# One chain of small matrices for two batches instead of two, and the whole instruction order replaced

## The chip, the cores and the metric

The kernel runs on one core of one Trainium2 chip. Its time is the device time of an execution in microseconds (us); the number that counts is the median over the runs of a kernel. The engines are TensorE (PE, matmuls and transposes through it; PEld is its weight loads), VectorE (DVE), ScalarE (ACT), GpSimd (POOL) and SyncE (SP, which here only issues DMAs).

## The reference

Four batches, four heads, 1088 tokens, head size 32. The first block is attention with a sketched second-degree kernel; its output, as a matrix of 1088 x 128 for each batch, goes through a second block that mixes tokens with two 1088 x 1088 matrices.

```python
a = einsum('rd,bhsd->bhsr', S1, x); b = einsum('rd,bhsd->bhsr', S2, x)      # x is q, then k; r = 8
phi(x) = einsum('bhsi,bhsj->bhsij', a, b)                                   # 64 features
kv = einsum('bhsf,bhsd->bhfd', phi(k), v);  z = sum of phi(k) over s
x = (phi(q) @ kv) / (phi(q) . z + 1e-6)                                     # heads side by side: 128 columns
theta = x @ w_theta
y = w_tok_r @ (x * cos(theta)) + w_tok_i @ (x * sin(theta))
u = x + y
out = u + max(u @ w_ch, 0)
```

The denominator can come close to zero, so the kernel forms it in two words (a rounded part and a rest). That is what most of the small matrices are for.

## The kernel before

**The plan.** The kernel does not issue its work as it is written. Each step is recorded by `op` (L133) as an operation: an engine (P, V, A, G, S for PE, DVE, ACT, POOL, SP), an assumed duration, a function that emits its instructions, and the tiles that it writes and reads. The string `ORDER` (L29 to L67) lists the numbers of all operations in one sequence, found outside the kernel by a search. `lay` (L207) goes through it once with the assumed costs; from that it takes which buffer of a class each tile gets (22 "big" tiles, 5 "zs", 8 PSUM banks and so on) and a start time for each operation. `issue` (L273) then emits the operations in that sequence, so each engine's instructions stand in the order of the string. Between the operations `first` and `last`, where the plan sees PE idle, it emits "spins" (`spin`, L434): matmuls on an idle tile whose result nobody reads, one for each 0.2 us of planned gap.

**The work.** For each batch b:

- `load` (L659) brings k, q and v in. For batches 1 to 3 k is loaded a second time (`loadh`, L720).
- `key_sums` (L683): the sum of squares of k (ACT), a grid for rounding, k rounded to bf16 (`keys`, DVE), the rest k minus rounded (DVE). For batches 1 to 3, POOL adds the rounded words into the second copy of k by an accumulating DMA (`join`, L396; big<-hf). PE then forms for each head the product of the rounded words (`sums`, 9 steps) and of the rests with that second copy (`rest`, 9 steps; batch 0 has two products there instead). ACT copies them out (`halves`).
- `chain` (L838): from these 32 x 32 matrices a chain of small steps, each a short hop from engine to engine: DVE `split` in two words, PE product with the sketch, ACT copy, DVE `split_t`, PE product with a block matrix (`second`), DVE `norms`, PE product with ones, DVE `cut` (11 instructions), POOL `whole`. Its result (tiles mv and mf) is needed by `levels`. A chain may take several batches side by side: the tiles are then wider and some steps have other forms.
- `kfeatures` (L769): transposes of k (kT), its features (kf), their outer product on DVE and the sum with v on PE (kv), nine chunks in three groups. `chain_out` (L955) spreads kv.
- `query_scale`, `query_slices` (L997, L1021): q transposed on PE (qT), scaled by ACT, cut into f16 and a rest on DVE (q0).
- `levels` (L1050): nine PE steps give the features of q; DVE forms the denominator (`den`).
- `outputs_x` (L1129): outer products of the features (DVE, num, L384 g<-lv), transposed on PE (L1155), copied by ACT (L1159), multiplied with kv; then theta, its phase on DVE, sine and cosine on ACT (L1197 to L1203) and the product z = x * (cos, sin) on DVE.

Each of the 17 blocks of token weights (`row`) is loaded as 64-bit words and turned into fp32 by two ACT and two DVE instructions (L646 to L654). Batches 0 and 1 are mixed row by row (`mix`, PE). Batches 2 and 3 share a form with seven products (`winograd`, products 1 to 7; POOL adds weight blocks by DMA, L1328). Each output is finished with one more matmul and stored by SP, in four DMAs of 32 partitions (L1283) or, for the last 128 columns, in one (L1297).

**What the change touches.** `CHAINS` (L71) lists the batches that go through a chain together: batch 0 alone, batch 1 alone, 2 and 3 together. The loop near the end of the kernel goes through it: for the entry with batch 0 the features of k come after the chain, and `last` (the last operation before which spins are emitted) follows it. `read_small` (L452) loads the two sketch matrices; the plan gives that load a cost of 0.25. Right at the start, ACT runs one Sin on a tile `warm` (L444), before which its function table is loaded.

Of the kernel before, what the change touches and what calls it, by code (L numbers as in the profile page):

```python
# [26 lines left out]
TINY = 2.0**-60  # L27
UP = 256.0
ORDER = """  # L29
    0 1 35 12 5 13 10 11 107 14 53 15 16 18 54 108 57 55 101 19 58 20 47 48 59 17 3 4 60 61 62 63 64 65 66 38 67  # L30
    68 21 138 142 125 50 144 36 102 79 95 69 49 70 71 56 72 40 73 74 22 80 81 309 96 311 147 23 51 75 24 126 145
    7 250 257 261 28 127 82 39 97 128 129 251 98 25 8 99 103 310 143 312 104 105 139 76 77 78 140 31 263 192 193
    146 41 307 308 166 84 119 120 32 85 33 37 131 266 313 109 86 148 149 267 132 150 151 110 111 167 168 314 186
    100 344 268 269 152 153 87 88 205 209 345 106 112 154 244 9 347 113 133 187 42 188 134 26 264 89 2 245 34 90
    91 189 43 285 135 198 199 194 195 141 92 93 155 238 156 157 270 271 272 273 158 274 159 160 161 262 162 163
    6 211 164 165 286 287 121 239 29 122 27 114 190 315 123 346 171 348 200 201 94 364 424 116 428 425 426 429
    432 214 233 427 215 216 359 202 430 44 360 169 431 433 434 435 234 235 288 236 252 316 206 333 172 436 117
    366 327 124 437 438 196 45 253 173 207 210 439 328 217 118 174 175 440 317 339 83 441 442 365 325 170 176
    326 443 318 319 320 321 191 130 136 115 444 334 177 331 265 178 445 323 197 453 52 137 240 324 246 446 341
    241 332 30 213 247 179 203 204 180 335 336 454 460 449 322 46 340 450 447 218 219 242 220 221 222 258 275  # L40
    276 342 277 278 279 448 456 455 457 349 394 451 248 458 212 452 280 350 343 351 259 181 467 281 535 536 469
    531 470 537 532 463 459 533 282 283 534 527 528 529 538 461 530 539 223 224 225 226 227 228 254 464 476 183
    540 182 462 229 230 231 468 471 465 352 473 541 472 474 466 184 284 542 232 475 477 478 543 353 354 544 355
    243 545 546 547 548 484 249 255 256 549 356 384 483 492 493 485 185 386 361 479 480 556 481 260 486 494 385
    552 553 550 551 357 559 560 557 558 554 563 561 555 571 562 208 564 565 482 358 362 367 487 374 566 567 578
    570 572 489 289 573 574 575 576 363 488 368 329 579 369 495 290 568 580 569 581 370 371 496 497 375 291 577
    292 582 586 490 641 642 643 491 588 377 583 293 589 372 376 584 618 619 595 585 294 620 295 296 297 644 645
    379 646 380 381 621 590 622 596 623 373 419 330 396 395 592 591 298 498 668 669 670 303 382 421 383 671 672
    673 674 675 378 664 665 420 397 237 300 404 387 666 587 593 409 422 597 388 598 647 648 649 650 411 624 594
    423 406 305 410 405 389 667 398 412 676 599 600 601 602 299 301 391 407 413 408 390 603 604 499 392 393 399  # L50
    400 401 500 414 306 836 402 403 415 677 651 652 678 501 502 416 679 417 503 504 505 506 302 680 418 507 681
    508 515 682 683 840 509 337 684 685 688 690 338 686 687 730 726 727 731 732 728 521 729 865 722 723 724 653
    304 835 654 510 869 733 605 625 839 626 627 628 629 691 725 834 689 692 693 734 735 736 694 695 737 696 655
    630 631 738 739 740 741 742 743 632 698 746 748 697 699 744 747 700 656 701 511 512 705 657 707 703 749 658
    708 709 702 711 745 606 633 713 750 751 704 752 753 516 814 815 715 706 795 796 797 816 710 714 607 513 712
    817 798 755 804 837 754 756 716 717 777 779 780 863 719 799 781 818 819 718 522 868 768 770 800 759 761 720
    771 772 805 762 820 757 782 763 806 774 838 867 841 773 807 808 809 810 811 758 721 760 634 767 769 514 764
    801 893 608 864 765 635 766 831 776 775 778 783 784 832 861 802 851 852 821 853 854 833 891 862 523 524 855
    856 822 857 803 860 880 858 785 525 926 889 881 882 890 859 907 894 866 883 884 885 659 892 636 886 786 929
    930 870 823 827 787 788 789 790 609 895 928 791 792 793 610 908 887 896 794 871 872 873 909 910 932 911 912  # L60
    874 875 876 877 517 518 913 914 888 915 828 931 842 965 933 916 934 843 844 845 927 878 879 948 846 847 949
    950 920 939 848 849 850 812 935 937 813 637 897 638 639 936 526 611 612 613 951 940 924 952 953 954 898 899
    900 901 902 964 938 941 942 943 944 829 640 955 903 956 519 824 520 825 826 977 987 988 925 660 945 946 947
    661 830 662 663 960 904 905 966 989 614 906 615 967 968 969 616 961 617 921 917 918 919 970 971 972 973 957
    974 922 923 975 990 962 978 979 991 958 959 976 997 998 992 980 993 999 994 995 963 1000 996 981 982 983 984
    985 986 1006 1008 1007 1009 1001 1002 1010 1003 1004 1005
"""  # L67
WARM = 0
FILL = 5.0
SPINS = 8  # L70
CHAINS = ((0,), (1,), (2, 3))  # L71
QPOOL = (False,) * 4
KEEP = (2, 3)
KEEP_CLS = "big"
# [245 lines left out]
def kernel(  # L320
# [13 lines left out]
    S, DM = out.shape[1], out.shape[2]  # L334
# [122 lines left out]
    if wide:  # L457
        st = fixed((NS,), I64, "st")
        y = fixed((NS,), I32, "sy")
        z = fixed((NS,), I32, "sz")  # L460
        op("V", 0.1, lambda: V.memset(st().bitcast(F32), 0.0), [st], [])
        op("S", 0.25, read_small, [st], [], lk=3)

        def words():
            w = st().bitcast(I32).rearrange("p (n t) -> p n t", t=2)
            return w[:, :, 0], w[:, :, 1]

        op("A", 0.25, lambda: A.activation(sp()[:, 0], words()[1].bitcast(F32), AF.Prelu, scale=2.0**-112,
                                           alpha=-(2.0**32)), [(sp, 0)], [st])

        def unpack():
            wl = words()[0]
            x = sp()[:, 0].bitcast(I32)
            ts(x, x, 3, ALU.logical_shift_left)
            stt(x, wl, 29, x, ALU.logical_shift_right, ALU.bitwise_or)
            ts(y(), x, -(1 << 23), ALU.bitwise_and)
            ts(z(), wl, 0x1FFFFFFF, ALU.bitwise_and)

        op("V", 0.85, unpack, [(sp, 0), y, z], [st], lk=2)
        op("A", 0.25, lambda: A.activation(sp()[:, 1], z(), AF.Copy, scale=2.0**-52), [(sp, 1)], [z])  # L480
        vop(NS, lambda: tt(V, sp()[:, 1], sp()[:, 1], y().bitcast(F32), ALU.mult), [(sp, 1)], [y])
    else:
        op("V", 0.2, lambda: V.memset(sp(), 0.0), [sp], [])
        op("S", 0.25, read_small, [(sp, 0)], [], lk=3)

    def powers(mfn, m, n, name):

# [1013 lines left out]
```

## Time and profile before

| | us |
|---|---|
| runs | 221.52, 222.49, 222.84 |
| median | 222.49 |
| the profiled execution | 222.86 |
| its span, first to last instruction | 221.1 |
| PE busy | 212.8 |
| DVE busy | 167.0 |
| ACT busy | 114.9 |
| granted PE clock | 1.000 of full speed |

The span is the time between the first and the last instruction; some 1.8 us of the execution lie around it. Lines are given as in this kernel (L384 and the like); in the changed kernel all lines stand one lower. A line can be that of a helper: L404 is any matmul, L384 any DVE or POOL instruction with two tensors. Matmuls overlap and their ends are modelled, so a busy PE need not be PE at its peak.

### The profile page before, as it was taken

Reading aid. Unit: us, or ns where it says so; the run is one execution under the profiler, and the core shown is the slowest. Engines: PE = TensorE matmul, PEld = TensorE weight load, DVE = VectorE, ACT = ScalarE, POOL = GpSimd, SP = SyncE. Lnnn points to the kernel's source line nnn. Section 1 sums busy time; section 2 is a strip of 40 time slices with the busy share of each in tenths; the row PEclk is TensorE's granted clock in tenths of the full one; section 3 lists DMA queues with packets and bytes.
Section 4 is the critical chain, followed back from the end, with each engine's and each line's share of the span. In section 5 each row is a group of like instructions: output and inputs, shape, how many; then the busy total and the mean of one; then the engine's idle time right before and its main releaser. Section 6 shows DMA issues by size and latency. Waiting matters only on the chain.

```text
span 221.1 us, 5129 instructions
## 1 busy us (share of the span) xinstructions
PE 212.8 (96%) x2066; PEld 160.8 (73%) x2066; DVE 167.0 (76%) x360; ACT 114.9 (52%) x237; POOL 45.5 (21%) x81
## 2 busy tenths in 40 slices
PE   7999998999999999999999999999999999999993
PEld 3786987777776757686666685778888787788772
DVE  2899897999899999899999969953899005324951
ACT  3988657989699798949740042377930000000000
POOL 1168260101200000100040083000273165030000
PEclk9999999999999999999999999999999999999999
DMA  6999999985509008948862069411098489772673
GB/s 183 411 424 319 394 418 362 418 270 211 205 9 369 30 0 268 373 170 260 345 115 41 0 104 178 73 20 20 0 185 139 80 149 180 122 111 34 100 115 69
DMA packets 26987, 40.19 MB, mean 182 GB/s; under 512 B 18260, under 2 KB 19284, under 8 KB 24788
## 3 DMA queue, kind: packets, MB, share of 16 engines
q1 hardware_dynamic: 22212, 30.30, 40.0%
q0 software_dynamic: 4752, 9.57, 24.4%
q8 instruction: 16, 0.26, 0.4%
q14 instruction: 7, 0.06, 0.1%
HBM read 28.07 MB, written 2.23 MB: 137 GB/s over the span
## 4 chain that ended last, share of the span: by engine, by line
PE 80%; DVE 5%; ACT 5%; SPq 3%; DMA 3%; issue 2%
PE ps L404 73%; SPq L1283 3%; DMA big<-k_l 2%; PE ps L1188 2%; PE ps L1155 2%; PE ps L792 2%; ACT big L649 2%; PE ps L435 1%; DVE lv L384 1%; DVE g L384 1%; DMA out<-g 1%; PE ps L1035 1%; ACT big L699 1%; DVE big L391 1%; ACT big L1003 1%
## 5 line engine op out<-in xcount | busy, mean ns | idle before, releaser
L404 PE MATMUL ps<-big,zs 128*128 128x384 f32 (+4 forms) x366 | 102.8, 426 | 0.4 <-DVE big L384 0.4
L404 PEld LDWEIGHTS ps<-big,zs 128*128 128x128 f32 x366 | 65.6, 190 | 27.6 <-DVE big L384 1.6
L1267 ACT COPY g<-ps 128x384 f32<-128x384 f32 (+1 forms) x6 | 2.6, 464 | 44.6 <-DVE g L1279 32.0
L384 DVE CUSTOM_DVE_ANT_0 big<-big,big 128x2176 uint16<-128x2176 uint16 x17 | 21.5, 1285 | 0.3
L647 ACT ACTIVATE big<-zs 128x1088 f32<-128x1088 f32 x17 | 20.6, 1215 | 2.3 <-DMA zs<-w_tok 1.8
L649 ACT ACTIVATE big<-zs 128x1088 int32<-128x1088 uint32 (+1 forms) x18 | 20.8, 1167 | 1.1 <-DVE big L384 1.1
L404 PE MATMUL ps<-mf,big 128*128 128x96 f32 x72 | 14.6, 296 | 0.9 <-issue 0.9
L384 DVE TENSOR_TENSOR zs<-ps,g 128x768 f32<-128x768 f32 (+2 forms) x20 | 12.3, 629 | 3.6 <-ACT g L1201 2.2
L391 DVE SCALAR_TENSOR_TENSOR big<-ps,even,big 128x256 f32<-128x256 f32 (+1 forms) x10 | 4.8, 493 | 12.6 <-PE ps L404 12.6
L404 PE MATMUL ps<-big,big 128*32 128x32 f32 (+2 forms) x320 | 14.1, 220 | 0.2 <-issue 0.2
L1328 POOL DMA_DIRECT2D big<-zs x8 | 7.0, 1132 | 34.7 <-PE ps L404 29.4
L1328 POOL DMA_DIRECT2D big<-big x8 | 9.2, 1638 | 19.7 <-issue 19.7
L404 PEld LDWEIGHTS ps<-big,big 128*32 128x32 f32 (+1 forms) x320 | 10.3, 118 | 3.4 <-issue 1.5
L398 POOL DMA_DIRECT2D g<-big x6 | 7.8, 1433 | 23.4 <-ACT g L1267 23.4
L1295 ACT COPY g<-ps 128x128 f32<-128x128 f32 x2 | 0.5, 265 | 23.0 <-PE ps L1293 22.0
L388 DVE TENSOR_SCALAR big<-big 128x1088 int32<-128x1088 int32 x17 | 12.1, 719 | 0.0
L404 PEld LDWEIGHTS <-hf 128*32 128x32 bf16 (+1 forms) x252 | 10.8, 99 | 1.7 <-issue 0.5
L435 PE MATMUL ps<-idle 128*128 128x384 bf16 x39 | 10.6, 398 | 1.3 <-POOL idle L437 1.3
L404 PEld LDWEIGHTS ps<-mf,big 128*128 128x128 f32 x72 | 10.9, 191 | 1.1 <-issue 1.1
L384 DVE TENSOR_TENSOR g<-lv 128x768 f32<-128x768 f32 x12 | 11.1, 953 | 0.3
L404 PE MATMUL ps<-w,big 128*128 128x128 f32 x76 | 10.9, 280 | 0.4 <-ACT g L1295 0.4
L404 PEld LDWEIGHTS ps<-w,big 128*128 128x128 f32 x76 | 9.9, 192 | 1.5 <-ACT g L1295 0.6
(199 smaller groups left out, 399.6 us busy)
## 6 DMA issues: line engine op xcount, KB each, us to landing
zs<-w_tok SPq DMA_DIRECT2D x17, 1088.0 KB, 5.6
big<-k_l SPq DMA_DIRECT2D x7, 576.0 KB, 8.1
big<-q_l SPq DMA_DIRECT2D x4, 576.0 KB, 15.6
big<-v_l SPq DMA_DIRECT2D x4, 576.0 KB, 8.0
big<-big POOLq DMA_DIRECT2D x8, 272.0 KB, 6.1
big<-zs POOLq DMA_DIRECT2D x8, 272.0 KB, 3.9
zs<-big POOLq DMA_DIRECT2D x8, 272.0 KB, 5.7
big<-hf POOLq DMA_DIRECT2D x3, 576.0 KB, 9.9
```

The costliest lines, as they stand in the source:

```text
L384: eng.tensor_tensor(out=o, in0=a, in1=b, op=f)
L388: (eng or V).tensor_scalar(out=o, in0=a, scalar1=s1, scalar2=s2, op0=op0, **kw)
L391: (eng or V).scalar_tensor_tensor(out=o, in0=a, scalar=s, in1=b, op0=op0, op1=op1)
L398: op("G", 1.05, lambda: G.dma_start(dst(), src(), accum_op=ALU.add), w, r, chan=chan)
L404: T.matmul(o, lhs, rhs, start=start, stop=stop, skip_group_check=True)
L435: T.matmul(nowhere(), idle()[:, 0:P], idle(), start=True, stop=True, skip_group_check=True)
L647: op("A", 0.22 + n * 0.0009, lambda: A.activation(dfn(), words_of(raw(), n)[1].bitcast(F32), AF.Prelu, scale=2.0**-112, alpha=-(2.0**32)), ...
L649: op("A", 0.22 + n * 0.0009, lambda: A.activation(stp(), words_of(raw(), n)[0].bitcast(U32), AF.Copy, scale=2.0**-29), [stp], [raw])
L792: T.transpose(tr()[:, i * P:(i + 1) * P], kx()[:, g * GC + i].rearrange("p h d -> p (h d)"), ident())
L1155: T.transpose(tr()[:, i * P:(i + 1) * P], qp()[:, i * H + 2 * n:i * H + 2 * n + 2].rearrange("p h i j -> p (h i j)"), ident())
L1283: SY.dma_start(out[b, t0 - o:t0 + w, f * SQ:(f + 1) * SQ].rearrange("(c j) i -> j c i", j=SQ), ot()[f * SQ:(f + 1) * SQ, :o + w].rearrange ...
L1328: op("G", 1.05, lambda i=i: G.dma_start(dst[0](i), x[0](i), accum_op=ALU.add), [dst[1](i)], [x[1](i)], chan=ADD_FLY3)
```

## The change

```diff
 ORDER = """
-    0 1 35 12 5 13 10 11 107 14 53 15 16 18 54 108 57 55 101 19 58 20 47 48 59 17 3 4 60 61 62 63 64 65 66 38 67
...
+    0 1 35 53 12 13 14 2 10 38 126 57 15 16 58 17 18 54 59 132 127 138 7 84 151 60 61 62 63 88 64 19 20 65 85 21
...
-CHAINS = ((0,), (1,), (2, 3))
+CHAINS = ((0, 1), (2, 3))
...
-        op("S", 0.25, read_small, [st], [], lk=3)
+        op("S", 0.9, read_small, [st], [], lk=3)
...
-        op("S", 0.25, read_small, [(sp, 0)], [], lk=3)
+        op("S", 0.9, read_small, [(sp, 0)], [], lk=3)
```

Batches 0 and 1 go through one chain. Since operations are numbered as they are recorded, the numbers of the new string name other operations than those of the old one; the sequence is a new one throughout. The cost of the small load only enters the plan.

What the built programs hold, before and after: PE 39 and 42 spins, and four matmul calls fewer in the chain; DVE 362 and 345 instructions; ACT 229 and 225, among them one table load before and two after; POOL 86 and 84; SP the same 79. All other instructions are the same in number and form. The order of the loads on SP:

```
before: k0 small w2 k1 q0 k3 k2 k1again q1 v0 row1 q2 q3 k3again row5 row4 v1 v2 k2again row0 v3 row2 row11 ...
after:  k0 small k1 k1again q0 k3 k2 q3 w2 q1 q2 row1 v0 row0 row2 v1 row9 v2 k3again row5 k2again v3 row6 ...
```

The first operations on POOL (the number is the batch; "join" is the accumulating DMA):

```
before: idle grid0 blocks scaled square2 join1 sliced square2 grid1 blocks sliced chain0 join3 blocks join2 chain1 ...
after:  idle blocks grid0 join1 scaled square2 sliced grid1 sliced square2 blocks chain(0,1) blocks join2 join3 ...
```

PE up to batch 0's levels, without the repetitions:

```
before: kT0 sums0 kT1 rest0 qT0 kT3 kf1 kf0 rest0 kT2 qT0 kT1 sums3 kf0 chain0 sums1 kT2 kv0 kT3 kf1 kf2
        chain0 kT2 kf2 chain0 kT3 rest1 sums3 kf1 qT1 kf2 levels0 ...   (chain1 follows behind levels0)
after:  kT0 kT1 sums0 rest0 kT1 kf0 qT0 kf0 kf1 rest0 sums1 qT0 kf0 kT1 kT2 kf1 kT3 rest1 kf2 kT3 chain(0,1)
        kT2 qT3 chain(0,1) chain(0,1) kf2 kv0 kf1 kf2 kT3 levels0 ...
```

At the end PE had the 128-column parts of product 4 mixed with the others; in the new order the part for columns 288 to 416 comes alone, last. The Sin on `warm` is ACT's second instruction before, and stands behind 49 others after.

## The prediction

> **What bounds the kernel now.** I read the page first, then the chain of work that ended last, then the waits of TensorE (PE) and VectorE (DVE), then the timeline of the engines up to 92 us.
>
> ```profile
> span 221.1 us, 5129 instructions
> PE 212.8 (96%) x2066; PEld 160.8 (73%) x2066; DVE 167.0 (76%) x360; ACT 114.9 (52%) x237; POOL 45.5 (21%) x81
> ...
> PE   7999998999999999999999999999999999999993
> ...
> DVE  2899897999899999899999969953899005324951
> ```
>
> PE is busy almost throughout, so what can be won is time in which PE runs idle-tile spins (L435) or waits. The digits of DVE say where: 9 of 10 up to about 155 us.
>
> ```profile
> 46.29 0.38 DVE lv L384
> ...
> 46.69 1.83 DVE g L384 x2
> ...
> 70.42 0.48 ACT g L1159
> 70.90 0.04 issue
> 70.95 0.93 PE ps L1155 x6
> ...
> 98.86 40.96 PE ps L404 x230
> ```
>
> This is the chain, in order of time (start, us, what). From 37.5 to 48.7 us it is ACT and DVE work, and the last place in the body where PE is released by another engine is 70.95 us, the transposes of batch 1's second outer product. ACT's copy of the first product, which the chain names, ended at 70.90, DVE's second product (69.78 to 70.73) 0.17 us ahead of it: both hang on DVE's first. From there to about 209 us the chain is PE alone. So the body ends at: the time when DVE reaches that product, plus PE's work behind it.
>
> DVE's waits between 5 and 71 us (who, for whom: us in total, times, longest), and the line of sums of the windows from 5.28 to 70.73 us:
>
> ```profile
> DVE sm L388 <- PE ps L404: 1.3, 1, 1.3
> DVE sm L915 <- PE ps L404: 0.7, 1, 0.7
> DVE big L388 <- ACT lv L1068: 0.6, 1, 0.6
> DVE sm L388 <- ACT big L699: 0.3, 1, 0.3
> ```
>
> ```profile
> sum 65.45, PE 62.80 PEld 50.79 DVE 60.04 ACT 55.51 POOL 17.34; mean PE 15.70 PEld 12.70 DVE 15.01 ACT 13.88 POOL 4.34
> ```
>
> The waits are 2.9 us in all; DVE is busy 60.0 of 65.5 us, and the rest is small steps between its instructions.
>
> **The change, part by part.** *The merged chain.* On DVE, batch 0's chain took 17.70-19.23, 23.05-23.72, 26.55-26.91 and 27.72-30.03 (timeline): 4.9 us. Batch 1's took 33.04-34.26, 41.65-42.34, 45.98-46.29, 48.44-50.66: 4.4 us. The chain of two batches that the trace has (2 and 3) took 79.90-81.69, 84.78-85.78, 88.07-88.45, 88.92-91.46: 5.7 us.
>
> ```profile
> 28.72 0.19 DVE L391 SCALAR_TENSOR_TENSOR sm<-sm,sm 128x32 f32<-128x32 f32 x1
> ...
> 89.94 0.23 DVE L391 SCALAR_TENSOR_TENSOR sm<-sm,sm 128x64 f32<-128x64 f32 x1
> ```
>
> The reader sees why: twice the width costs 0.04 us more, a second instruction 0.19. The merged chain of 0 and 1 needs one subtraction more than that of 2 and 3 (batch 0 keeps its third product), 0.23 us: 5.9 us. DVE has 9.3 - 5.9 = 3.4 us less to do (17 instructions fewer). By the instruction order of the two programs, DVE has ahead of batch 1's second outer product the same work but for the chain (-3.4 us), one phase subtraction of theta that now stands ahead (0.55 us row, 0.5 us start to start) and small scalars (0.1): 2.8 us less.
>
> *PE.* Four matmul calls (eight instructions) go, about 0.12 us each from start to start (six with the block matrix in 0.59 us, two with the ones in 0.25, and 0.1 in the small ones, which now stand in one row): 1.0 us less. Three spins come, 0.16 us each: 0.5 us more. All of this is ahead of the point, where PE waits for DVE, so I count it at nothing; if DVE's lag were gone it would be worth -0.5 us. Behind the point both programs hold the same PE work (the sequences there are reordered, not changed).
>
> *The wait that the merge adds.* Batch 0's levels now need batch 1's key products too, so also its second product, whose operand is k of batch 1 loaded a second time, to which POOL adds the rounded words by DMA. Order on the changed queues: SP loads that second copy fourth instead of eighth, POOL issues the addition fourth instead of sixth, ahead of the slices of the sketch matrices, which queue behind it (they need DVE's rounding of those, which I put at 14 us: no cost).
>
> ```profile
> big<-hf POOLq DMA_DIRECT2D x3, 576.0 KB, 9.9
> ```
>
> That is the page's row of these additions: 9.9 us from issue to landing; this one was issued at 15.47 us.
>
> DVE's rounded words of batch 1, which POOL waits for, ended at 11.18 us before; in the new order the rounding of batch 0 and the same scalars stand ahead of it, so I take 12 us for the issue and, by the row, 21.9 us for the landing. PE comes to these products at 20 us by the work ahead of them alone (start to start, from 5.5 us), at some 22 with the waits of the first 15 us. Then copy, split, and the four steps of the chain: batch 0's took 16.0 to 32.2 us with other work between; here the same four round trips fit 22 to about 32.5. So levels of batch 0 start as before, and DVE's idle time is taken as the same 2.9 us. Bounds: 1 us (the 1.3 us wait at 37.62 and the 0.7 us one go) to 6 us (landing as late as PE first read that buffer before, 28.2).
>
> *PE's instructions.* The four waits "issue" of PE (2.2 us) sit at almost even counts:
>
> ```profile
> PE ps L404 <- issue: 2.2, 4, 0.9
> ```
>
> ```profile
> 0.00:21.60 21.60, 19.95 (x346) 14.85 (x346) 16.12 (x61) 16.53 (x47) 9.41 (x31) 1.00 0.91 335
> 0.00:28.60 28.60, 26.02 (x471) 20.42 (x472) 22.20 (x78) 21.07 (x57) 11.51 (x35) 1.00 0.94 349
> 0.00:34.30 34.30, 31.60 (x599) 25.36 (x599) 27.41 (x96) 24.77 (x67) 15.22 (x44) 1.00 0.95 359
> 0.00:47.70 47.70, 43.94 (x852) 35.80 (x852) 39.21 (x124) 36.92 (x96) 16.08 (x45) 1.00 0.98 365
> ```
>
> The second fence counts PE and PEld instructions up to the start of each wait. Together: 692, 943, 1198, 1704, steps of 251, 255, 506. [...] In the new order the first such border falls into batch 1's second products, the next into batch 0's key-value sums, the third near the end of its levels. I take the same 2.2 us, beside DVE's lag as before; bounds 0 and 4.4 (each border hit twice as hard). [...]
>
> *ACT.* Five instructions fewer, but the Sin that warmed the table at 0.72 us now stands behind 49 ACT instructions, and the built program holds a second table load there. The row: 1.28 us and 0.20 us for the Sin. It falls just ahead of the copies of batch 0's levels; ACT is busy 55.5 of 65.5 us in this stretch, and DVE does some 7 us of other work between the chain and the first use of the levels, so I take 0; bounds 0 and 1.5. [...]
>
> *Loads.* SP moves v of batch 0 behind one weight row, q 2 and q 3 (2.3 MB more ahead, 6 us at 360 GB/s; some 22 us, wanted at about 29). Weight rows 0 and 2 go ahead of the other v; the second copy of k 2 now waits for the buffer of a weight step that DVE frees at about 37 us, so additions 2 and 3 land at some 52 and 56 us by the 9.9 us row, close to their use: 0 here, bound 2 us. The cost of the small load in the plan (0.25 to 0.9) is no instruction.
>
> *The tail.* The last product's 128-wide part now comes alone at the end. Before, 4.6 us lie between its last matmul (about 216.5) and the end; one finish less stands in line there, but a 288-column store with its four issues (0.5 us each by SP's rows from 209 to 216 us in the chain) stands ahead of the last store on SP: 0, bounds -0.5 and +0.5.
>
> **Sum.** Span 221.1 - 2.8 = 218.3 us. The profiled execution took 222.86 us, 1.76 more than its span, and the median of the three runs, 222.49, is 0.37 under it: 218.3 + 1.76 - 0.37 = 219.7 us.
>
> **Rivals.** *R1, the lag moves elsewhere.* PE shows only 0.2 us of waiting for DVE or ACT up to 71 us besides "issue"; if the borders of its instructions or the additions for batches 2 and 3 (52 and 56 us) hold it instead, most of the 2.8 us is returned and only PE's own 0.5 remains: 222.0 us. For it: PE busy in 23.74 of the 24.04 us before 70.73. Against: the chain turns to DVE and ACT in 37 to 49 us, and spins count as busy.
>
> *R2, more than forecast.* The chain is done once instead of twice, so DVE's waits of 1.3 and 0.7 us around it go too: 217.7 us. For it: both waits are for PE, which has room. Against: the new wait at 22 us.
>
> *R3, slower.* The addition for batch 1 lands late. All of batch 0's levels, and with them DVE's work behind, hang on it from now on. Price one for one. The gain is gone if it lands after 24.7 us, over 1% slower if after 27; at 28.2 (where PE read it before) 219.7 + 6.3 = 226.0 us. For it: DMA is at 1.02 of its engines from 5 to 18 us. Against: 9.9 us is measured in just that load.
>
> **How the numbers follow.** Forecast (218.5 to 221.0) 0.50; R1 (221.0 to 223) 0.26; R2 (under 218.5) 0.11; R3 (over 223) 0.13. One per cent, about what a measurement of this kernel can tell from no change, is 2.2 us: faster means under 220.3. About three quarters of the forecast's share and all of R2 are under that: 0.48. Over 224.7 lies most of R3: 0.11. Within: 0.41. The range leaves out the lower half of R2 and most of R3: 218.0 to 223.3; the forecast's own is 218.5 to 221.0.
>
> **What would show it.** Right: DVE's chain is one group of 128x64 forms before levels of batch 0, of 5.9 us; levels of batch 0 start at 31 to 33 us; the first row of weights is multiplied at 60 to 62 us instead of 64.4; the transposes of batch 1's second outer product come at 67 to 69. Wrong: DVE waits over 2 us for PE's products of batch 1 around 22 to 27 us (R3), PE waits over 1 us on an addition or "issue" after 45 us (R1), or ACT's second table load stands on the chain of work.

## The result and the profile after

| | before | changed |
|---|---|---|
| median, us (21 runs each) | 222.15 | 223.61 |
| lowest and highest, us | 220.96, 223.00 | 222.60, 228.42 |
| the profiled execution, us | 222.86 | 223.37 |
| its span, us | 221.1 | 221.6 |

The ratio is 1.0071, with a 95% interval of 1.0053 to 1.0090: the change costs about 1.6 us. The forecast was 219.7 us in a range of 218.0 to 223.3. In four of the 21 executions of the changed kernel the mean granted clock was 0.966 to 0.985; the ratio leaves these four out, medians and highest times do not.

The page after, with the lines that answer to the first fence of the prediction:

```profile
span 221.6 us, 5090 instructions
...
PE 211.4 (95%) x2061; PEld 159.0 (72%) x2061; DVE 164.1 (74%) x343; ACT 115.5 (52%) x233; POOL 44.1 (20%) x79
...
PE   7998899989999999999999999999999999999991
```

PE is busy 1.4 us less, DVE 2.9 us less, and the span is 0.5 us longer: work went, idle time came. The chain of work that ended last says where (start, us, what):

```profile
11.25 11.02 DMA big<-hf
...
30.45 1.28 ACT L443
...
43.31 13.63 DMA big<-hf
...
56.98 1.49 PE ps L403 x50
...
200.73 0.59 DVE g L1278
201.34 0.32 SPq L1282
```

Before, this chain was PE with ACT and DVE steps, and from 209.31 us SP, which issues the stores. Now two of POOL's additions stand on it for 24.65 us, and SP from 201.34 us. The waits of PE from 5 to 71 us (who, for whom: us in total, times, longest):

```profile
PE ps L403 <- DMA big<-hf: 2.0, 3, 1.3
PE ps L1154 <- DVE g L383: 1.1, 1, 1.1
PE ps L403 <- DVE sm L383: 0.6, 2, 0.4
```

"Issue", 2.2 us before, is gone from PE's row, and these three rows, 3.7 us in all, are new: the additions (waits that end at 22.3, 54.9 and 57.0 us), DVE's first outer product of batch 0 (46.6 us), the steps of the merged chain. A fourth new row has 0.2 us. DVE's and PE's sums from 5.28 us to DVE's second outer product of batch 1 follow, first of after (product at 68.79 us), then of before (69.78 us):

```profile
sum 63.51, PE 59.54 PEld 47.93 DVE 57.88 ACT 53.98 POOL 15.92; mean PE 59.54 PEld 47.93 DVE 57.88 ACT 53.98 POOL 15.92
```

```profile
sum 64.50, PE 61.87 PEld 50.14 DVE 59.09 ACT 54.56 POOL 17.34; mean PE 61.87 PEld 50.14 DVE 59.09 ACT 54.56 POOL 17.34
```

DVE got there 0.99 us sooner: 1.21 us less busy, 0.22 us more idle. But PE did not follow at once. The transposes of batch 1's first outer product are a good mark, since both programs have by then issued the same PE work but for the chain and the spins (in the tables the start of the fourth of them): 70.21 us before, 70.02 us after, 0.2 us gained. Right behind it, first before, then after:

```profile
69.89 0.82 PE L1155 MATMUL ps<-ident,g 128*128 128x128 f32 x6
70.95 0.93 PE L1155 MATMUL ps<-ident,g 128*128 128x128 f32 x6 [0.24 <-ACT g L1159]
71.81 1.51 PE L404 MATMUL ps<-g,sm 128*64 128x384 f32 x8
```

```profile
69.69 1.61 PE L1154 MATMUL ps<-ident,g 128*128 128x128 f32 x12
71.22 1.54 PE L403 MATMUL ps<-g,sm 128*64 128x384 f32 x8
```

The wait of 0.24 us at 70.95 is gone, which from start to start is worth 0.4 us: the next products come at 71.22 instead of 71.81 us. So the front gave 0.2 us at the mark and 0.6 us behind it.

At the end (timeline, SP and DVE), first before, then after:

```profile
217.76 1.02 SPq L1297 DMA_DIRECT2D out<-g  x2
218.11 0.29 DVE L391 SCALAR_TENSOR_TENSOR g<-ps,g 128x128 f32<-128x128 f32 x1 [0.38 <-DMA out<-g]
```

```profile
216.37 0.45 SPq L1296 DMA_DIRECT2D out<-g  x1
216.92 1.88 SPq L1282 DMA_DIRECT2D out<-g  x4
217.68 0.29 DVE L390 SCALAR_TENSOR_TENSOR g<-ps,g 128x128 f32<-128x128 f32 x1 [0.94 <-DMA out<-g]
218.90 0.40 SPq L1296 DMA_DIRECT2D out<-g  x1
```

Before, the data of the last store were ready at 218.40 us and SP issued it at 218.43. Now they are ready at 217.97 us, 0.43 us sooner, but SP issues the store at 218.90: four issues of another store stand ahead. So the span's 0.5 us are 0.4 gained up to the last data and 0.9 lost on SP. Why the four are so late stands in SP's waits from 195 us on:

```profile
SPq L1282 <- DVE g L1278: 51.5, 1, 51.5
```

SP waited for batch 0's second part while batch 1's third part, ready at 186.69 us, stood behind it in the queue. From 201.34 us SP then issues 34 times in a row, one each 0.53 us, up to the last store (before: 30 times, from 202.48 us).

### The profile page after: what moved, and what is told of

It reads as the page before. It is cut to its first block, busy times and chain, and to the rows that moved or that the text cites. A ratio compares the mean times of both kernels' runs of the same rounds, so it can differ in the third digit from the quotient of the medians.

```text
span 221.6 us, 5090 instructions
## 1 busy us (share of the span) xinstructions
PE 211.4 (95%) x2061; PEld 159.0 (72%) x2061; DVE 164.1 (74%) x343; ACT 115.5 (52%) x233; POOL 44.1 (20%) x79
## 4 chain that ended last, share of the span: by engine, by line
PE 65%; DMA 16%; SPq 6%; DVE 5%; ACT 3%; issue 2%; POOL 0%; POOLq 0%; DVEq 0%
PE ps L403 62%; DMA big<-hf 11%; SPq L1282 6%; DMA big<-k_l 4%; PE ps L1187 2%; DVE sm L383 1%; PE ps L1154 1%; ACT big L646 1%; DMA out<-g 1%; DVE sm L387 1%; DVE hf L387 1%; ACT L443 1%; DVE big L383 1%; ACT big L648 1%; ACT lv L1067 0%
## 5 line engine op out<-in xcount | busy, mean ns | idle before, releaser
L646 ACT ACTIVATE big<-zs 128x1088 f32<-128x1088 f32 x17 | 20.5, 1214 | 4.7 <-DMA zs<-w_tok 4.4
L648 ACT ACTIVATE big<-zs 128x1088 int32<-128x1088 uint32 (+1 forms) x18 | 21.4, 1192 | 2.7 <-DMA zs<-w_tok 1.9
L403 PE MATMUL ps<-big,big 128*32 128x32 f32 (+2 forms) x320 | 13.2, 218 | 2.0 <-DMA big<-hf 2.0
L390 DVE SCALAR_TENSOR_TENSOR g<-ps,g 128x384 f32<-128x384 f32 (+2 forms) x8 | 3.8, 472 | 13.8 <-PE ps L403 12.7
L1327 POOL DMA_DIRECT2D big<-big x8 | 8.7, 1536 | 25.6 <-issue 16.9
L403 PEld LDWEIGHTS ps<-big,big 128*32 128x32 f32 (+1 forms) x320 | 9.7, 117 | 5.2 <-DMA big<-hf 2.3
L434 PE MATMUL ps<-idle 128*128 128x384 bf16 x42 | 11.5, 388 | 1.3 <-POOL idle L436 1.3
L1327 POOL DMA_DIRECT2D big<-zs x8 | 6.9, 947 | 28.2 <-PE ps L403 28.2
L397 POOL DMA_DIRECT2D g<-big x6 | 8.7, 1498 | 14.1 <-ACT g L1266 14.1
L383 DVE TENSOR_TENSOR big<-big,hf 128x1152 f32<-128x1152 f32 x8 | 10.8, 1352 | 0.1
L403 PEld LDWEIGHTS ps<-mf,big 128*128 128x128 f32 x72 | 10.9, 191 | 0.0
```

The source lines that it names most:

```text
L383: eng.tensor_tensor(out=o, in0=a, in1=b, op=f)
L390: (eng or V).scalar_tensor_tensor(out=o, in0=a, scalar=s, in1=b, op0=op0, op1=op1)
L397: op("G", 1.05, lambda: G.dma_start(dst(), src(), accum_op=ALU.add), w, r, chan=chan)
L403: T.matmul(o, lhs, rhs, start=start, stop=stop, skip_group_check=True)
L434: T.matmul(nowhere(), idle()[:, 0:P], idle(), start=True, stop=True, skip_group_check=True)
L646: op("A", 0.22 + n * 0.0009, lambda: A.activation(dfn(), words_of(raw(), n)[1].bitcast(F32), AF.Prelu, scale=2.0**-112, alpha=-(2.0**32)), ...
```

## The experiments

All times in this table are starts in the profiled execution of each kernel, in us: the products of batch 1's rests, batch 0's levels (the chunk that comes first in the kernel before; in the changed order it is the fifth), PE's mark at the end of the front, the issue of the last store, and the span. The last column is the ratio of times to before with its interval.

```
                rests1  levels0    mark  last store   span   ratio
before           28.22    32.18   70.21     218.43   221.1
changed          22.31    35.29   70.02     218.90   221.6   1.0071 [1.0053, 1.0090]
dve_less         27.95    31.78   69.81     218.02   220.6   1.0016 [0.9993, 1.0039]
pe_less          27.86    31.89   69.17     218.16   220.8   0.9997 [0.9973, 1.0020]
front_new        22.87    37.18   71.82     221.11   223.8   1.0120 [1.0082, 1.0159]
rear_new         28.34    32.23   69.72     219.82   222.5   1.0100 [1.0065, 1.0136]
store_first      21.99    35.04   69.83     217.78   220.4   1.0066 [1.0032, 1.0099]
spin_more        22.76    35.83   71.02     219.89   222.6   1.0141 [1.0089, 1.0194]
pe_less_act      28.37    32.10   68.82     217.04   219.7   0.9969 [0.9944, 0.9994]
both_less_act    28.10    31.92   69.20     217.42   220.1   0.9960 [0.9932, 0.9988]
rests_late       21.61    34.73   68.13     216.06   218.7   0.9980 [0.9947, 1.0014]
warm_early       22.99    35.72   70.35     218.30   220.9   1.0031 [1.0008, 1.0055]
joins_early      22.25    37.22   71.47     219.41   222.0   1.0005 [0.9972, 1.0037]
best             22.78    35.51   68.65     216.58   219.2   0.9958 [0.9929, 0.9987]
filled           23.62    37.23   70.39     218.38   221.0   0.9993 [0.9962, 1.0024]
```

**Is DVE's arrival the bound?** (dve_less; in the kernel before)

```diff
-        vop(2 * NT, lambda: tt(V, fl(0, 2), fl(0, 2), sl(0, 2), ALU.subtract), [lv], [(sx, 0)], lk=1)
+        vop(2 * NT, lambda: b == 1 or tt(V, fl(0, 2), fl(0, 2), sl(0, 2), ALU.subtract), [lv], [(sx, 0)], lk=1)
...
-        op("V", n * 0.00053 + 0.15, lambda: ts(dfn().bitcast(I32), dfn().bitcast(I32), 3, ALU.logical_shift_left),
+        op("V", n * 0.00053 + 0.15, lambda: cut or ts(dfn().bitcast(I32), dfn().bitcast(I32), 3, ALU.logical_shift_left),
...
-        op("V", n * 0.00112 + 0.08, lambda: tt(V, dfn().bitcast(I32), dfn().bitcast(I32), stp(), ALU.add), [dst],
+        op("V", n * 0.00112 + 0.08, lambda: cut or tt(V, dfn().bitcast(I32), dfn().bitcast(I32), stp(), ALU.add), [dst],
```

The last two edits stand in `weight`; `cut` is true for row 2 alone.

> The kernel before, with three VectorE instructions left out that work in place (den of batch 1, its second instruction, 0.75 us; the two that finish weight row 2, 0.72 and 1.28 us). Part of the output is therefore not the reference's. All three stood ahead of batch 1's second outer product, so DVE has 2.75 us less to do there, as much as I forecast for the change; order, buffers and spins stay. Theory A (the prediction's: the time when DVE reaches that product sets the end): 2.7 us less, about 219.4 us, ratio 0.988. Theory B (PE has no room of its own up to there, and DVE's lag costs no more than the 0.24 us that PE waited at 70.7): 0 to 0.3 us less, ratio 0.9985 to 1.000.

No gain, ratio 1.0016. The trace is exact: the mark is 0.40 us earlier than before, but those 0.4 us are there at batch 0's levels already (31.78 against 32.18), 27 us ahead of the first instruction left out. DVE reached batch 1's second outer product at 67.58 instead of 69.78 us, and PE still waited for ACT there, as before; now DVE waited for PE (waits from 69 to 72 us):

```profile
DVE g L384 <- PE ps L1155: 1.9, 1, 1.9
PE ps L1155 <- ACT g L1159: 0.2, 1, 0.2
```

Taking out 2.75 us of DVE bought nothing: theory A, the foundation of the forecast, is wrong. The chain of waits of the kernel before had said so, for ahead of ACT's copy at 70.42 us it names 6.7 us of ACT's own work and no DVE:

```profile
63.76 0.37 ACT g L827
64.14 1.13 ACT big L649
...
69.31 1.11 ACT big L647
```

**Is it PE?** (pe_less, and later both in one)

```diff
-                    mm(o[:, 2 * HR:], x, m[:, 1], False, False)
-                    mm(o[:, 2 * HR:], x, m[:, 2], False, False)
+                    if b != 1:
+                        mm(o[:, 2 * HR:], x, m[:, 1], False, False)
+                        mm(o[:, 2 * HR:], x, m[:, 2], False, False)
```

> The kernel before, with 18 of the matmuls of batch 1's levels left out (two of three f16 products in each of nine steps, 0.1 us each by the rows, 1.8 us in all; part of the output is not the reference's). All lie between 50 and 60 us, ahead of batch 1's second outer product; DVE's and ACT's work is the same. Theory A (DVE's arrival at that product sets the end): 0 to 0.2 us less, ratio 0.999 to 1.000. Theory B (PE's own work sets the end): 1.5 to 1.8 us less, about 220.5 us, ratio 0.992 to 0.993.

The mark comes 1.04 us earlier, 0.29 of it from ahead of the place. The other 0.75 us are all that the 18 matmuls cost: a step of the levels, which has three such products, took 0.39 us from start to start and takes 0.30 with one. First before, then this run:

```profile
54.06 0.29 PE L404 MATMUL ps<-mv,hf 128*128 128x96 f16 x3
54.19 0.43 PE L404 MATMUL ps<-mf,big 128*128 128x96 f32 x2
54.45 0.29 PE L404 MATMUL ps<-mv,hf 128*128 128x96 f16 x3
```

```profile
53.70 0.21 PE L404 MATMUL ps<-mv,hf 128*128 128x96 f16 x1
53.74 0.43 PE L404 MATMUL ps<-mf,big 128*128 128x96 f32 x2
54.00 0.21 PE L404 MATMUL ps<-mv,hf 128*128 128x96 f16 x1
```

That is 0.04 us for each matmul, and not the 0.1 us that I expected. What was left out of PE came back in full, and every product from 58 us to the last one comes 1.0 us earlier than before (0.4 us in dve_less). So theory B holds, with a smaller size than I gave it. The time did not move, since the end of the span took it back: in this execution one of SP's issues took 1.71 us instead of 0.47, and the last store went 0.8 us after its data. To see behind that, three of the last stores went to ACT's queue:

```diff
-                SY.dma_start(out[b, t0 - o:t0 + w, f * SQ:(f + 1) * SQ].rearrange("(c j) i -> j c i", j=SQ),
+                (A if (b, t0 - o) in ACTQ else SY).dma_start(out[b, t0 - o:t0 + w, f * SQ:(f + 1) * SQ].rearrange("(c j) i -> j c i", j=SQ),
...
+ACTQ = ((2, 0), (1, 0), (3, 544))
```

> The kernel before with three of its last stores (12 of 30 issues, those of batch 2's first half, batch 1's first part and batch 3's second half) issued from ACT's queue instead of SP's. In the profiled execution the last store left SP 0.03 us after its data, SP had 0.4 us to spare. Theory C: 0 to 0.4 us less, ratio 0.998 to 1.000 (executions in which one issue on SP takes 1.2 us longer gain). Rival (ACT's queue slows the DMAs or ACT's last copies): slower, ratio over 1.002.

> The kernel that leaves out 18 matmuls of batch 1's levels (so part of the output is not the reference's), with the same three stores on ACT's queue. In its trace the last product was 1.05 us earlier than before, and the last store left SP only 0.24 us earlier, 0.8 us behind its data. Theory C (SP's queue took that gain): 0.8 to 1.1 us less than before, ratio 0.995 to 0.997. Rival (the gain is lost elsewhere, or the one execution was an exception): as without ACT's queue, ratio 0.999 to 1.000.

The kernel before with the stores on ACT's queue: 0.9979 (0.9953 to 1.0005), inside what theory C allowed. With the matmuls left out as well: 0.9969, 0.7 us under before, and 0.2 us under the former alone, with intervals that overlap. Here too one of SP's issues took 1.61 us, but with twelve issues fewer on SP the last store went 0.03 us after its data, 1.4 us earlier than before.

> The kernel before without the three VectorE instructions (2.75 us) and without the 18 matmuls (1.8 us), both left out in earlier runs one at a time, so part of the output is not the reference's; three of the last stores go out on ACT's queue, so that SP does not hide the result. In the traces the last product came 0.4 us earlier for the first alone and 1.05 us for the second alone. Theory F (PE and DVE wait for each other in turns, neither alone is the bound): more than the sum, 1.7 to 2.5 us less than before, ratio 0.989 to 0.992. Rival (PE alone is the bound up to 70 us): as with the matmuls alone, about 1.0 us less, ratio 0.995 to 0.997.

The mark is at 69.20 us, as with the matmuls alone (69.17); ratio 0.9960 (0.9932 to 0.9988). Theory F falls, its rival stands: DVE brings nothing on top of PE.

**Front or rear?** Orders put together from both programs, cut at PE's mark (front_new, in the changed kernel's numbers; rear_new, in those of before; of each edit the first place is shown):

```diff
-... 539 540 543 537 538 469 344 546 547 ...
+... 539 540 543 537 381 373 247 538 344 546 547 ...
```

```diff
-... 385 552 553 550 551 357 559 560 557 ...
+... 385 552 553 550 289 369 487 489 551 ...
```

> The changed kernel's order up to the products of batch 1's first numerators (70.02 us in its trace, 70.21 in the trace of before, by when both have issued the same PE work but for the chain), and from there on the order of before. Theory C (the loss lies behind that point, at the end above all): the front gains the 0.2 us of the traces, ratio 0.999. Rival D (the front loses, by run to run differences that the two profiled executions do not show): 0.7 to 1.5 us more, ratio 1.003 to 1.007.

> The counterpart: two chains and the order of before up to the same point, the changed kernel's order behind it. Theory C: it carries the loss: at the end the last store leaves SP 0.45 us later than before (four issues of the store ahead of it), and with the 0.2 us that the traces show lost between 70 us and the last product 0.6 us or more, ratio 1.003 to 1.008. Rival D: no loss, ratio 0.999 to 1.001.

Both halves alone are slower than the whole change, so this sum does not come out and the pair is inconclusive on its own. The traces show two things nevertheless. Rear_new has the end that theory C named: its last store goes at 219.82 us, 0.94 us after its data. At the seam, at 72.2 us, its PE also waits 0.9 us for ACT, which neither whole order does. Front_new is late at batch 0's levels already (37.18 us): in this execution the clock was at a half for 3.4 us from 30.7 us on. That is worth up to half of 3.4 us, an estimate, and is told last.

**SP's queue at the end** (store_first, in the changed kernel's order)

```diff
-... 928 929 913 507 930 953 941 ... 909 601 650 934 602 ...
+... 928 929 913 650 507 930 953 941 ... 909 601 934 602 ...
```

> The changed kernel with one number moved: the store of batch 1's third part (its data are ready at 186.69 us) goes ahead of the store of batch 0's second part on SP, behind which it stood for 18 us. Theory C (the tail is held by SP, which issues the last 33 stores in 18 us without a pause, the last of them 0.92 us after its data at 217.97): four issues of 0.5 us leave the queue, the last store goes with its data, 0.9 us less than the changed kernel, ratio to before about 1.003. Rival (the tail is held by the last products, or by the DMAs themselves): no change, ratio 1.007.

The timeline of its end, to be held against that of the changed kernel:

```profile
215.75 1.87 SPq L1288 DMA_DIRECT2D out<-g  x4
...
217.46 0.29 DVE L396 SCALAR_TENSOR_TENSOR g<-ps,g 128x128 f32<-128x128 f32 x1 [0.94 <-ACT g L1300]
217.78 0.35 SPq L1302 DMA_DIRECT2D out<-g  x1
```

The last store now goes 0.03 us after its data, and the span is 220.4 us, 1.2 less, of which 0.2 stood ahead already. So the trace shows theory C's 0.9 us. The ratio of 1.0066 does not: the runs scatter from 221.9 us up, and the interval holds 1.003 as well as 1.007. The next runs stand on this order.

**The additions for batches 2 and 3** (rests_late, on store_first)

```diff
-... 169 210 329 ... 446 262 263 525 264 521 330 265 266 267 268 341 ... 453 211 527 ... 531 532 212 347 ...
+... 169 329 ... 446 525 521 330 341 ... 453 527 ... 531 532 210 211 262 263 264 265 266 267 268 212 347 ...
```

> The same base, with PE's first products of the rests of batches 2 and 3 (which wait 0.2 and 0.7 us at 54.9 and 57.0 us for the additions) moved behind the first weight row of the mix at 62 us. Theory B (PE's own work and waits set the end): the 0.9 us of waits go, 0.5 to 0.9 us less than the base, span 219.5 to 219.9. Rival (PE then waits for DVE's features of batch 0 or 1 instead, DVE being the bound): 0 to 0.2 us less.

Better than expected: from 1.0066 to 0.9980, and the span from 220.4 to 218.7 us. At 53.3 us PE was as far as in store_first (within 0.04 us), at the mark it was 1.70 us ahead: all of it was gained behind 53.3 us, where the reads stood. The waits of PE from 45 to 70 us, first of store_first, then of this kernel:

```profile
PE ps L409 <- DMA big<-hf: 0.8, 2, 0.6
PE ps L1160 <- DVE g L389: 0.6, 1, 0.6
```

```profile
PE ps L1160 <- DVE g L389: 0.9, 1, 0.9
```

The same products in the timeline, first of store_first, then of this kernel:

```profile
54.68 0.27 PE L409 MATMUL ps<-big,big 128*32 128x32 f32 x8 [0.24 <-DMA big<-hf]
...
56.80 0.70 PE L409 MATMUL ps<-big,big 128*32 128x32 f32 x56 [0.57 <-DMA big<-hf]
...
59.02 0.27 PE L409 MATMUL ps<-big,big 128*32 128x32 f32 x8
...
64.37 0.83 PE L409 MATMUL ps<-big,big 128*32 128x32 f32 x72
```

```profile
62.07 1.43 PE L409 MATMUL ps<-big,big 128*32 128x32 f32 x144
```

The order of all other engines is the same. Counted from start to start, the two reads had cost 1.05 us more than their own work; 0.4 us more came from the 144 small products, which now stand in one piece and take 1.36 us instead of 1.78 us in four; some 0.2 us are spread over small steps. So the early reads were the main hold on the front, and with them gone the changed kernel passes the mark 2.1 us ahead of before.

**Why so late?** (joins_early, on store_first)

```diff
-... 227 328 249 233 ...     ... 315 197 306 307 46 ...
+... 227 328 197 249 233 ... ... 315 306 307 46 ...
```

> The base with the store moved ahead on SP, and on SP the second copy of k of batch 2 loaded ahead of that of batch 3 and of weight row 5 instead of behind them. PE's order is untouched. Theory G (the additions are late because that load waits for a buffer until 37.4 us, and POOL issues the addition for batch 3 behind that for batch 2): both are issued at about 38 us instead of 42.7 and 43.3, land at 48 to 52 us, PE does not wait for them at 55 and 57: as much as the late reading of the rests brought, 1.2 to 1.7 us less than the base, span 218.7 to 219.2. Rival (the additions themselves take longer in this load, 13.6 us from issue to landing as the second did, or row 5 is now late): 0 to 0.5 us less.

The ratio is 1.0005, 0.6% or 1.35 us under that of store_first (the intervals still touch), as much as theory G expected. Its way is only half right: the additions were issued at 40.2 and 41.4 us instead of 43.7 and 44.4, not at 38, and took 12.3 and 15.9 us to land. The order of the loads is one part of the lateness, the duration of the addition the other. In this execution PE did not wait for them, but it came to them later (the clock was at a half from 30.6 to 34.1 us), so it cannot say how much room was left.

**The second table load** (warm_early, on store_first)

```diff
-... 125 221 11 160 ...
+... 14 2 10 11 38 ...
```

> The changed kernel with the store of batch 1's third part moved ahead on SP (as in the run of that name, which serves as its base: span 220.4 us where the clock was full), and the Sin on the warm tile back at its old place as ACT's second instruction, so that there is one table load instead of two. Theory (the prediction's: the second load of 1.28 us and the Sin of 0.20 us at 30.4 to 31.9 us lie beside other work, since PE is busy throughout 30 to 35 us): 0 to 0.3 us less than the base, span 220.1 to 220.4. Rival (the chain of waits, on which the load stands, is right to put it there): 1 to 1.5 us less, span 219 to 219.4.

The span was 220.9 us, not under 220.4; PE came 1.0 us later to the rests of batch 1 (22.99 against 21.99 us, the addition landed that much later), 0.7 us later to batch 0's levels and 0.5 us later to the mark. Counted from the rests, 0.3 and 0.5 us were gained, not the 1.5 us of load and Sin, though the chain of waits goes through both. The ratio, 1.0031, is lower than store_first's 1.0066, but the intervals overlap; a gain of under 1 us is not excluded.

**The merge without the new order** (merge_alone, a single execution; its order is that of before but for the steps pulled ahead)

```diff
-CHAINS = ((0,), (1,), (2, 3))
+CHAINS = ((0, 1), (2, 3))
```

> The merge of the chains alone: one chain for batches 0 and 1 with the order of before; only the steps that the merged chain needs (batch 1's rounding on POOL and its products on PE) are pulled ahead of it. Batch 0's levels then wait for the addition for batch 1, which is still issued at 15.5 us. Price of lateness by the prediction's third rival (one for one behind levels of batch 0, which I expect at 40 to 43 us instead of 32.2): 6 to 10 us more, 228 to 232 us. Rival (the rest of the order has room for it): under 225 us.

239.43 us. The addition was issued at 15.80 us, PE read it at 25.83, and batch 0's levels began at 50.17 instead of 32.18 us; the mark came 16.7 us late (86.88), the end 16.6. The price is nearly one for one, as the third rival said. The levels' own 18 us are more than I expected. The clock was at a half from 30.7 to 51.2 us; and the chain's last step on DVE ended at 44.60 us, but PE had ten idle matmuls (46.97 to 50.38 us) ahead of the levels, because the plan put them there. How much each of the two costs was not separated.

**More idle matmuls, real products instead, and all repairs together.**

```diff
+EXTRA = {102: 9, 121: 4, 123: 3}
...
-                    for _ in range(int((o.start - last - 0.08) * FILL)):
+                    for _ in range(max(0, int((o.start - last - 0.08) * FILL)) + EXTRA.get(o.i, 0)):
```

> The changed kernel with 16 more idle matmuls (0.16 us each): nine ahead of the products of batch 1's rests, which wait there 1.4 us for the addition, four and three ahead of the second and third step of the chain, where PE waits 0.6 and 0.4 us. Theory E (in part of the executions the gaps of PE between 21 and 30 us bring the granted clock down to a half for a few us behind them, as the profiled execution of the mixed order with the new front shows at 30 to 34 us; that is the 0.9 us by which the median of the changed kernel stands further from before than its profiled execution does): granted clocks back at 0.998 to 1.000, no time over 225 us, median 0.6 to 1 us under the changed kernel, ratio 1.002 to 1.004. Rival (the clock has another cause, or costs nothing in the median): ratio 1.007 or, where the addition lands early, up to 1.010.

> As the kernel with the three repairs, and three of PE's products moved ahead into its gaps around the merged chain: a transpose of k of batch 3 ahead of the rests of batch 1, the first key-value product of batch 0 ahead of the chain's second step, a feature product of batch 2 ahead of its third. Theory (gaps of PE without real products between 21 and 30 us let the clock fall at about 30 us, and PE sets the end): no time that shows the lower clock (all within 1.5 us of the fastest), and 0.3 to 1 us less than with the three repairs alone. Rival (the fall of the clock has another cause, and DVE's chain, which does not get sooner, sets the end): as often disturbed, no difference in the rest.

> The changed kernel with the three repairs together: the store moved ahead on SP, PE's first rests of batches 2 and 3 behind the first row of the mix, the Sin on the warm tile back at the start. Theory: what the merge brings comes out when both holds are gone: as with the rests moved (220.3 to 221.5 us where the clock was full), the table load adds 0 to 0.3 us; median 220.5 to 221.3, ratio 0.993 to 0.997. Rival (the lower clock takes it back): over 0.998.

Filled, on the kernel with the three repairs (best):

```diff
-... 231 102 300 301 ... 49 237 220 ... 120 121 136 ... 122 123 334 124 326 181 131 137 ...
+... 231 237 102 300 301 ... 49 220 ... 120 131 121 136 ... 122 181 123 334 124 326 137 ...
```

Best holds the edits of store_first, rests_late and warm_early and no others.

Theory E falls: with the idle matmuls the ratio is 1.0141, the mark 1.0 us later, and three of six executions still had a mean clock of 0.98 to 0.99. Filled was not faster than best either: levels begin 1.7 us later (37.23 against 35.51), the mark 1.74 later, the span 1.8. That is the price of one for one once more, this time at full clock. But the trace does not put it down to the moved products alone: the addition for batch 1 landed at 23.58 instead of 22.73 us, which is half of it, and the other half is a wait "issue" of 0.82 us within the moved key-value products, ahead of the chain's second step. Its clocks fell too (mean 0.977 and 0.982 in two of twelve executions). Best is faster than before: 220.98 us, ratio 0.9958 (0.9929 to 0.9987). It is the only kernel with the whole computation whose interval lies under 1.

## Why the prediction was wrong

The span came out at 221.6 us instead of 218.3, and the median stood 0.24 us over the profiled execution instead of 0.37 under it: 3.3 and 0.6 us, together the 3.9 us between 219.7 and 223.6. Of the 3.3 us, 2.2 were missing behind the front (0.6 gained instead of 2.8), 0.2 were lost on the way to the last data and 0.9 on SP. The 0.6 us are the places of the two profiled executions among their runs: that of before stands 0.71 us over the median of its 21 runs, that of the changed kernel 0.24 us under.

- *"The body ends at the time when DVE reaches that product, plus PE's work behind it."* This is the step that failed. It rested on the reading that ACT's copy and DVE's second product "both hang on DVE's first". But PE began the first transposes at 69.89 us without a wait, behind its own weight row, and ACT came to its copy out of its own work. PE had been idle 0.24 us at that place (0.4 us from start to start), and that much was to be had. Dve_less took out as much DVE work as I counted and gained nothing; pe_less took out 0.75 us of PE, and that came back in full at the mark and at the last product. So PE's own work and waits set the end. Among kernels of one order the end then follows the start of batch 0's levels: 1.7 us later in filled than in best, the end 1.8.
- *The merged chain, 5.9 us:* right, 5.95 us on DVE (23.49 to 31.93 in four pieces). *2.8 us less for DVE:* mis-sized, 1.2 us less busy, 0.99 us sooner. The 3.4 us for the chain were lengths with the small pauses between its instructions; busy it was 8.0 of 9.3 us before and 5.2 of 5.95 after, 2.8 us less.
- *Levels at 31 to 33 us, as before:* 33.66 for the first of them. The addition for batch 1 was well forecast (issued 11.25, landed 22.27 us; I had 12 and 21.9), the four round trips behind it took 0.9 us longer than the 10.5 I had. *First mix row at 60 to 62:* 62.63. *Transposes at 67 to 69:* 70.34.
- *Loads, "52 and 56 us, close to their use: 0 here, bound 2 us":* they landed at 54.8 and 56.9, and the choice of 0 within the bounds was wrong. Moving the reads was worth 1.7 us, 1.05 of it the reads themselves. The levels of batch 1 that stand behind a read on PE came later with it: in the trace of after the step behind the read at 54.93 us began 0.98 us after the step ahead of it, the next two 0.40 and 0.39 us apart. This was rival R1's mechanism; the sign that I had set for it, over 1 us of waiting on an addition after 45 us, was too high: the two waits show 0.7 us. It would have been tested by asking, for each late landing, which instruction of PE reads it and what stands behind.
- *The tail, "0, bounds -0.5 and +0.5":* the store that I named is what stands ahead of the last one, and store_first measured 0.9 us. I counted the four issues and not SP's backlog behind a store that waited 51.5 us.
- *PE's instruction borders, 2.2 us:* gone from PE's row here; 1.3 and 1.5 us in joins_early and spin_more, inside the bounds. The even counts were those of four waits in one trace, and after has no such wait on PE's row; that the waits return at such counts is not shown. *The table load, 0:* as far as warm_early shows, 0 to 0.5 us, within its bounds. It stood on the chain of work, my third sign of being wrong, and yet it was not what held. In the trace of after the load starts at 30.45 us, 0.02 us behind a copy, and takes 1.28 us; the Sin starts 0.01 us behind it and takes 0.20.
- *R3:* its price is nearly right (merge_alone: levels 18.0 us later, the end 16.6) and its condition did not come about.

So the direction was right for the front alone: with the holds taken out the mark stands at 68.1 to 68.7 us, 1.5 to 2.1 us under before, and the products behind it 0.4 us more. That this is the merge's doing is not shown, since the order is a new one throughout. Nor is it shown through which work it comes, if not through DVE's. Three candidates are PE's calls (1.0 us less, against 0.5 us more of spins), what ACT does for the second chain, and PE's waits "issue" (2.4 us up to the mark before, none in rests_late and best; but they also come and go from kernel to kernel, 1.6 us in dve_less and 0.6 in rear_new). None was tried alone.

## What to carry to other kernels

Before a gain is booked at a link of the chain of waits, look at how much the waiting engine lost there from start to start, and follow the chain back to see whose work it names. What a matmul costs is also read from start to start: here rows of 0.2 us stood for 0.04 us each (pe_less). List every transfer that lands later than before with the first instruction that reads it, and put that instruction late in its engine's order. At the end, count the issues left in the storing queue and see whether a store that must wait stands ahead of one that is ready.

## What the runs showed of the hardware

*The granted clock stood at 1.00 or at 0.50 in these traces, and four stretches at 0.50 lasted one, two and six times 3.4 us.* In the profiled execution of front_new (windows of 1 us; the third number from the end is the clock):

```profile
27.00:28.00 1.00, 0.76 (x7) 0.43 (x5) 0.86 (x7) 1.00 (x2) 0.00 (x0) 1.00 1.00 409
28.00:29.00 1.00, 0.82 (x7) 0.79 (x8) 0.90 (x2) 1.00 (x2) 0.00 (x0) 1.00 0.95 397
29.00:30.00 1.00, 0.78 (x6) 0.48 (x5) 0.94 (x4) 0.36 (x1) 0.00 (x0) 1.00 1.00 416
30.00:31.00 1.00, 1.00 (x27) 0.93 (x29) 0.86 (x7) 0.32 (x1) 0.00 (x0) 0.85 1.04 433
31.00:32.00 1.00, 1.00 (x51) 1.00 (x44) 0.86 (x5) 1.00 (x1) 0.43 (x1) 0.50 1.03 419
...
34.00:35.00 1.00, 1.00 (x10) 1.00 (x9) 0.44 (x4) 0.51 (x3) 0.00 (x0) 0.95 0.93 371
```

It is 0.50 from 30.7 to 34.1 us, 3.4 us; in joins_early from 30.6 to 34.1, again 3.4 us; in before_act from 28.6 to 35.4, 6.8 us; in merge_alone from 30.7 to 51.2, 20.5 us. Stretches at 0.50 that the end of the span cuts off (in pe_less and store_first the window from 220 us on) are not among them. In front_new PE was busy 0.76, 0.82 and 0.78 of the three us from 27 to 30, ahead of the fall, and the longest gap in them was 0.4 us (27.8 to 28.2, by windows of 0.1 us). Sixteen more idle matmuls did not keep the clock up (spin_more: a mean of 0.980 to 0.990 in three of six executions), and real products did not either (filled: 0.977 and 0.982 in two of twelve); in merge_alone seven single or paired idle matmuls within the half clock did not end it, and ten in a row (47.0 to 50.4 us) stood right ahead of its end. Why such means are more frequent with the new order (0.966 to 0.985 in four of 21 executions) than with the old one (0.951 in one of 113 of the kernel before, in the series beside the experiments) is open.

*The accumulating DMA of 576 KB* took 9.3 to 10.9 us from issue to landing in the trace of before, 11.0 to 13.6 in that of after, up to 15.9 in joins_early, and 4.3 and 4.4 in merge_alone, where all queues together moved 134 and 193 GB/s meanwhile (in before, for its three additions, 329 to 389). A row of three of them, 9.9 us, was too narrow a base for it.

*An issue on SP* took 0.53 us on the mean of the last 34 in after, and in some kernels one took far more: 1.71 us in pe_less, 1.61 and 1.68 in the two kernels with the same matmuls left out and stores on ACT's queue, 1.37 in front_new, in all four the fourth issue of the same store.
